# Another choice of scheduling rules per stretch of the plan, for a two-layer attention and MLP kernel on one core

## The chip, the cores and the metric

The kernel runs on one core of one Trainium2 chip. The metric is device microseconds of one execution, as the median of several. A core has five instruction queues that run in order and meet through semaphores: TensorE (PE, matmuls; its weight loads are listed as PEld), ScalarE (ACT, activation functions), VectorE (DVE), GpSimd (POOL) and SyncE (SP, which only issues DMAs here).

## The reference

Two rounds of attention and MLP over one sequence of S = 2048 tokens, D = 512, H = 32 heads of 16, F = 1792. Both rounds use the same weights.

```
x = x + A(layernorm(x));  x = x + B(layernorm(x))      # twice
A: qkv = x @ wqkv;  p = softmax(q k^T / 4) per head;  o = p v;  o @ wo
B: gelu(x @ w1 + b1) @ w2 + b2                           # tanh gelu
```

## The kernel before

**Cells.** The scores of one head for 128 keys and 512 queries are a *cell*: one 32-row matmul into one bank of PSUM (`score`, the lambda on line 1432). There are 4096 of them. A *pass* is a group of eight heads and 512 queries; its cells are numbered by key tile `kt` (16 of 128 keys) and by `a`, which names the row group of PE that holds the heads. No maximum is subtracted in the softmax: exp is taken of the scaled score directly.

**Two ways to take an exp.** ACT does it by its table, for two or three cells in one instruction (`exps`, line 1879). For some cells VectorE does it instead: one multiply-add whose 16-bit integer result is read as a bf16 (`dfirst`, line 1601), followed by two 64-bit additions on GpSimd (`dchain`, lines 1691 and 1695), which make shifted copies; the four copies are multiplied with V and three scaled copies of V (`VC`, line 1363) and summed. Which key tiles may go this way is in `KD` (line 52), five of sixteen in each layer. A cell of these five that VectorE has not been given by the end of its pass is taken by ACT (`next_act`).

**The rest.** Line 1945 multiplies the exps with V and collects the sums of the softmax in a 17th column; `norm` divides. Line 647 (`quads`) holds the matmuls of all projections and of the MLP. Line 1155 moves the MLP's hidden values from PSUM with their bias, line 1176 is the gelu on ACT (two long ones per query chunk, so that the table of ACT is switched to gelu and back once per chunk), and in the last chunk line 1150 takes gelu straight from PSUM. The projections and the MLP of a chunk of 512 tokens run beside the scores of the next chunk. Fillers are matmuls whose result nobody reads (`filler`); the planner puts them where PE would otherwise pause.

**What sets the order.** All of it is decided when the program is built. `_Sched.run` keeps a clock for each engine, and many threads (one for scores, one for exps, one for products with V, and so on) offer their next operation with an assumed duration and a priority. It picks the operation that can start first, notes its assumed end, and appends it to that engine's queue, with the semaphore waits that its data need. The chip then runs each queue in that order, at whatever speed it has; only the order is fixed.

**The rules.** Twelve constants of this planner are *knobs*. `ORDERS` (line 94) lists values for all twelve; `PICKS` names one line of it for each stretch of 24 us of the planner's ACT clock, 60 in all:

```
def tune(self):
    k = min(int(self.clock["act"] // STRETCH), len(PICKS) - 1)
    if k != self.stretch:
        self.stretch = k
        globals().update(zip(KNOBS, ORDERS[PICKS[k]]))
        LATENCY["pe"] = PE
```

The knobs in which the lines that are picked differ:

- `PE`: the assumed delay between a matmul's end and the start of what waits for it.
- `PTURG`: with fewer free buffers for exps than this, the products with V get a better priority (`urge`, line 1920).
- `PTLOW`: with more free buffers than this, the products with V take VectorE's cells first (line 1928).
- `SWAP`: how late VectorE may be while it is still given a cell in one of the two spare banks that a third cell of ACT's could use (`attach`, line 1534).
- `SEVAC`: the priority of VectorE's moves out of PSUM other than exps.
- `DULOW`: with no more free VectorE buffers than this, products with V are started although some rows have nothing yet (line 1917).

The other six are the same in all lines that are picked: `TOL` and `DCELL` in `attach`, `EXT` in `extend`, `ALONE` in `solo`, `TAIL` and `OPENING` in `next_d`. `attach` gives VectorE a cell only together with a group of ACT's, when a bank is free within `TOL`; `next_d` offers no more of a pass once fewer than `TAIL` of its cells are left.

Of the kernel before, what the change touches and what calls it, by code (L numbers as in the profile page):

```python
# [110 lines left out]
)  # L111
STRETCH = 24
PICKS = (1, 13, 1, 1, 13, 13, 1, 2, 1, 13, 1, 13, 13, 1, 1, 14, 1, 13, 13, 13, 13, 11, 3, 1,
         1, 13, 13, 13, 13, 13, 13, 1, 13, 13, 13, 1, 13, 1, 1, 1, 1, 3, 13, 13, 5, 1, 13, 13,
         1, 0, 1, 1, 13, 13, 13, 13, 1, 1, 1, 13)
LOG2E = 1.4426950408889634
E_SCALE = 0.25 * LOG2E * 128
E_BIAS = 15992.765054484162
# [145 lines left out]
class _Sched:  # L264
# [1793 lines left out]
```

## Time and profile before

| | us |
|---|---|
| median of 3 runs | 1429.57 (1429.56 to 1430.48) |
| profiled execution | 1429.75 |
| its span, first to last instruction | 1427.9 |
| ACT busy | 1401.1 (98%) |
| PE busy, fillers included | 1385.5 (97%) |
| VectorE busy | 1216.6 (85%) |
| GpSimd busy | 997.9 (70%) |

The profile is one execution, read from the hardware's own records. In a row of a group stand line, engine, operation, what it writes and reads with the shapes, how often, then busy time and mean duration of one, then the idle time of the engine just before these instructions and what ended it. Successive instructions of an engine overlap, so a mean duration can be longer than the step from one to the next. The chain of waits follows the work that ended last back to its releasers. A row of a stretch gives its borders and length, busy times with counts in brackets, the granted clock of TensorE (1.00 is full), the share of the DMA engines and GB/s.

### The profile page before, as it was taken

What the parts mean: (1) busy time and instruction counts of PE and PEld (TensorE: products, weight loads), DVE (VectorE), ACT (ScalarE), POOL (GpSimd) and SP (SyncE); (2) the same over time, 40 slices, a digit from 0 to 9 for tenths busy, and PEclk for the clock granted to TensorE, in tenths of its full rate; (3) what the DMA queues carried; (4) which work ended last, traced back from release to release, by engine and by line L of the source; (5) the groups of instructions that cost most, each with busy time, mean ns of one, the idle gap of its engine ahead of it and who ended that gap; (6) DMA issues with size and microseconds to landing.
All of it is one profiled execution on the core that took longest, in us unless ns stands there. A gap on an engine that the chain in (4) does not pass through costs nothing.

```text
span 1427.9 us, 45603 instructions
## 1 busy us (share of the span) xinstructions
PE 1385.5 (97%) x19402; PEld 420.7 (29%) x19402; DVE 1216.6 (85%) x2293; ACT 1401.1 (98%) x1406; POOL 997.9 (70%) x1256
## 2 busy tenths in 40 slices
PE   8999999999999999999999999999999999999999
PEld 3222222222222222222222222222222222344346
DVE  7789999788997889987998678899869977898684
ACT  7999999999999999999999999999999999999995
POOL 1086988668786787876767667757767977788661
PEclk9999999999999999999999999999999999999999
DMA  6100001261121611115411161101162105421522
GB/s 176 45 2 2 2 16 39 62 183 54 46 39 53 187 60 39 39 31 157 119 39 46 53 187 59 31 14 33 39 189 79 32 24 168 145 32 40 175 75 89
DMA packets 145187, 103.47 MB, mean 72 GB/s; under 512 B 37084, under 2 KB 143964, under 8 KB 144988
## 3 DMA queue, kind: packets, MB, share of 16 engines
q1 hardware_dynamic: 144988, 100.57, 25.2%
q8 instruction: 156, 2.56, 0.8%
q14 instruction: 43, 0.35, 0.1%
HBM read 88.74 MB, written 4.19 MB: 65 GB/s over the span
## 4 chain that ended last, share of the span: by engine, by line
ACT 67%; PE 24%; DVE 7%; POOL 2%; issue 1%; ACTq 0%; POOLq 0%
ACT pt L1879 50%; PE ps L1945 8%; PE ps L1432 8%; PE ps L647 7%; ACT q L1879 4%; ACT g L1879 3%; ACT g L1176 3%; ACT v L1879 3%; DVE du L1601 3%; ACT kt L1879 2%; POOL du L1695 1%; DVE kt L1601 1%; PE ps L1420 1%; ACT L1879 1%; ACT L1176 1%
## 5 line engine op out<-in xcount | busy, mean ns | idle before, releaser
L1879 ACT ACTIVATE pt<-ps 128x1024 bf16<-128x1024 f32 (+1 forms) x1085 | 1091.2, 1168 | 1.3 <-PE ps L1432 0.4
L1601 DVE TENSOR_SCALAR du<-ps 128x512 uint16<-128x512 f32 x894 | 597.2, 684 | 112.5 <-PE ps L1432 107.9
L1432 PE MATMUL ps<-qp,kt 32*128 32x512 bf16 x4096 | 537.4, 384 | 18.5 <-ACT pt L1879 11.2
L1695 POOL INT64_ADD du<-du x454 | 464.6, 1025 | 72.9 <-DVE qp L1380 9.6
L1691 POOL INT64_ADD du<-du x454 | 273.6, 605 | 231.9 <-DVE du L1601 180.8
L1945 PE MATMUL ps<-du,vc 128*17 128x512 bf16 (+1 forms) x2979 | 360.3, 360 | 2.3 <-POOL du L1695 0.6
L1432 PEld LDWEIGHTS ps<-qp,kt 32*128 32x128 bf16 x4096 | 143.2, 91 | 569.6 <-ACT pt L1879 177.9
L1945 PE MATMUL ps<-pt,v 128*17 128x512 bf16 (+1 forms) x2621 | 306.5, 359 | 4.3 <-ACT pt L1879 2.7
L1945 PE MATMUL ps<-du,v 128*17 128x512 bf16 (+1 forms) x993 | 166.3, 360 | 3.6 <-DVE v L988 1.0
L647 PE MATMUL ps<-xf,wr 128*32 128x512 bf16 (+1 forms) x2272 | 162.0, 371 | 0.4 <-DMA xf<-pt 0.2
L1601 DVE TENSOR_SCALAR kt<-ps 128x512 uint16<-128x512 f32 x202 | 136.2, 683 | 22.0 <-PE ps L1432 20.6
L1945 PE MATMUL ps<-kt,vc 128*17 128x512 bf16 (+1 forms) x732 | 145.1, 344 | 0.8 <-POOL du L1691 0.8
L1945 PEld LDWEIGHTS ps<-du,vc 128*17 128x17 bf16 x2979 | 95.6, 89 | 81.4 <-issue 35.6
L1695 POOL INT64_ADD kt<-kt x104 | 105.3, 1013 | 15.7 <-DVE ra L797 3.8
L647 PE MATMUL ps<-wr,g 128*32 128x512 bf16 x1504 | 110.7, 383 | 1.1 <-ACT g L1176 1.1
L1945 PEld LDWEIGHTS ps<-pt,v 128*17 128x17 bf16 x2621 | 74.2, 88 | 79.1 <-issue 53.2
L1945 PE MATMUL ps<-v,vc 128*17 128x512 bf16 (+1 forms) x405 | 90.4, 351 | 0.1
L1155 DVE TENSOR_SCALAR g<-ps,hb1t 128x512 bf16<-128x512 f32 (+1 forms) x112 | 79.0, 706 | 10.2 <-PE ps L647 9.8
L1601 DVE TENSOR_SCALAR v<-ps 128x512 uint16<-128x512 f32 x116 | 78.2, 682 | 11.0 <-PE ps L1432 10.6
L1691 POOL INT64_ADD kt<-kt x104 | 62.3, 599 | 35.6 <-DVE kt L1601 17.2
L1879 ACT ACTIVATE q<-ps 128x1024 bf16<-128x1024 f32 (+1 forms) x78 | 82.0, 1128 | 0.0
L1945 PE MATMUL ps<-kt,v 128*17 128x512 bf16 (+1 forms) x334 | 79.4, 354 | 1.9 <-POOL du L1695 0.9
(108 smaller groups left out, 1462.4 us busy)
## 6 DMA issues: line engine op xcount, KB each, us to landing
wr<-in_B_w_dram SPq DMA_DIRECT2D x243, 256.0 KB, 3.1
wr<-in_A_wqkv_dram SPq DMA_DIRECT2D x24, 256.0 KB, 2.8
wr<-in_A_wo_dram SPq DMA_DIRECT2D x17, 256.0 KB, 3.0
x<-in_A_x_dram SPq DMA_DIRECT2D x7, 512.0 KB, 4.9
pt<-in_B_w_dram SPq DMA_DIRECT2D x13, 256.0 KB, 3.9
kept<-x SPq DMA_DIRECT2D x4, 512.0 KB, 3.1
x<-kept SPq DMA_DIRECT2D x4, 512.0 KB, 3.9
out_dram<-x SPq DMA_DIRECT2D x16, 128.0 KB, 2.9
```

What stands on the lines that cost most here:

```text
L647: return [lambda e, a=a: e.matmul(out[32 * a:32 * a + 32, :], lhsT=lhsT[:, 32 * a:32 * a + 32], rhs=rhs, start=start, stop=stop, tile_posi ...
L1155: yield _Op("dve", 0.21 + n / 966, lambda e, fc=fc, pb=pb: e.tensor_scalar(T["G"][:, fc, q], pb, T["HB1T"][:, fc:fc + 1], None, op0=ALU.ad ...
L1176: lambda e, g=g: e.activation(out=g, in_=g, func=ACT.Gelu_apprx_tanh), reads=gk, writes=gk, prio=2)
L1420: fns.append(lambda e, o=o, w=w, a=a, m=m: e.matmul(o, lhsT=w, rhs=rhs, start=start, stop=start, tile_position=(0, m * a)))
L1432: return (lambda e: e.matmul(o, lhsT=lhsT, rhs=rhs, start=True, stop=True, tile_position=(32 * a, 0)), ["K%d.%d.%d" % (l, gb, kt // 4), "Q ...
L1601: yield _Op("dve", 0.682, lambda e: e.tensor_scalar(u, self.bank(b), E_SCALE, E_BIAS, op0=ALU.mult, op1=ALU.add), reads=["B.%d" % b], writ ...
L1691: yield _Op("pool", 0.151 + 0.2176 * n, lambda e: e.int64_add(words(1, 1), words(0, 1), SHIFT * ONES), reads=key[0], writes=key[1])
L1695: yield _Op("pool", 0.143 + 0.4352 * n, lambda e: e.int64_add(words(2, 2), words(0, 2), 2 * SHIFT * ONES), reads=key[0] + key[1], writes=k ...
L1879: yield _Op("act", 0.052 + 0.4267 * n, lambda e, src=src, dst=dst: e.activation(out=dst, in_=src, func=ACT.Exp, scale=0.25), reads=["B.%d" ...
L1945: op.fns.append(lambda e, o=o, lhsT=q[0][0][m], rhs=q[0][1][:, n * m:n * m + n], a=a, st=st, sp=sp: e.matmul(o, lhsT=lhsT, rhs=rhs, start= ...
```

## The change

Eight lines of `ORDERS` that no stretch picks are taken out, so the remaining ones get new numbers (old 5, 11, 13 and 14 become 4, 5, 6 and 7), and `PICKS` is replaced. By values, 31 of the 60 stretches get another rule than before: those numbered 1, 4, 5, 7, 10 to 15, 17, 21, 22, 24, 29, 30, 32, 33, 43 to 49 and 52 to 57. Rule 1 (`PE` 0.2175, `PTURG` 6) goes from 24 stretches to 31, and rule 6 (`PE` 0.219, `PTURG` 5) from 29 to 20. The new picks were found by running the program in order with disturbed durations of loads, matmul groups and gelus. Nothing else differs: no operation, shape, buffer or assumed duration of an operation.

```diff
     (0.219, 0.7, 99, 2, 0.2, 0.2, 6, 5, 0.68, 3.5, 10, 18),
-    (0.219, 0.45, 99, 2, 0.2, 0.2, 6, 5, 0.68, 3.5, 10, 18),
     (0.219, 0.55, 99, 2, 0.5, 0.2, 6, 5, 0.68, 3.5, 10, 18),
-    (0.219, 0.55, 99, 2, 0.35, 0.2, 6, 5, 0.68, 3.5, 10, 18),
-    (0.219, 0.55, 99, 2, 0.2, 0.1, 6, 5, 0.68, 3.5, 10, 18),
...
     (0.219, 0.55, 99, 2, 0.2, 0.2, 6, 4, 0.68, 3.5, 10, 18),
...
     (0.219, 0.55, 99, 2, 0.2, 0.2, 5, 5, 0.68, 3.5, 10, 18),
     (0.219, 0.55, 99, 1, 0.2, 0.2, 6, 3, 0.68, 3.5, 10, 18),
-    (0.2205, 0.6, 99, 2, 0.2, 0.2, 6, 5, 0.68, 3.5, 10, 18),
 )
 STRETCH = 24
-PICKS = (1, 13, 1, 1, 13, 13, 1, 2, 1, 13, 1, 13, 13, 1, 1, 14, 1, 13, 13, 13, 13, 11, 3, 1,
-         1, 13, 13, 13, 13, 13, 13, 1, 13, 13, 13, 1, 13, 1, 1, 1, 1, 3, 13, 13, 5, 1, 13, 13,
-         1, 0, 1, 1, 13, 13, 13, 13, 1, 1, 1, 13)
+PICKS = (1, 1, 1, 1, 1, 1, 1, 6, 1, 6, 5, 5, 1, 6, 6, 1, 1, 1, 6, 6, 6, 1, 6, 1,
+         5, 6, 6, 6, 6, 1, 1, 1, 1, 1, 6, 1, 6, 1, 1, 1, 1, 3, 6, 1, 6, 6, 3, 1,
+         3, 6, 1, 1, 5, 1, 3, 1, 6, 3, 1, 6)
```

The columns of a line are `PE, SWAP, EXT, DULOW, SEVAC, TOL, PTURG, PTLOW, DCELL, ALONE, TAIL, OPENING`.

4 rows, old and new, of the table ORDERS are left out of this document.

## The prediction

> **What bounds the kernel now.** I read four views in this order: the page's busy shares, three stages cut at the first and at the last exp, the groups that make up the exps on both engines, and eight stretches that each hold one eighth of the scores.
>
> ```profile
> span 1427.9 us, 45603 instructions
> PE 1385.5 (97%) x19402; PEld 420.7 (29%) x19402; DVE 1216.6 (85%) x2293; ACT 1401.1 (98%) x1406; POOL 997.9 (70%) x1256
> ```
>
> ACT and PE both look full, but PE is padded with matmuls put into its gaps (the fillers), so its share says little. The stages decide it:
>
> ```profile
> core 0: us, PE busy (x) PEld busy (x) DVE busy (x) ACT busy (x) POOL busy (x), PEclk, DMA share, GB/s
> 0.00:13.00 13.00, 9.51 (x163) 4.92 (x163) 7.78 (x29) 4.46 (x7) 3.83 (x16) 1.00 0.88 269
> 13.00:1401.40 1388.40, 1352.36 (x18669) 400.17 (x18672) 1197.48 (x2236) 1385.41 (x1383) 992.96 (x1238) 1.00 0.26 71
> 1401.40:1427.90 26.50, 23.59 (x577) 15.58 (x568) 11.34 (x30) 11.25 (x18) 1.15 (x2) 1.00 0.17 51
> ```
>
> Columns: the stretch and its length, each engine's busy time with its instructions, the granted clock, the DMA share. Between the first exp at 13.0 and the last at 1401.4, ACT is busy for 1385.41 of 1388.40 us: 2.99 us idle in 1388. So an order can shorten this stage in two ways only: give ACT less to do, or take some of these 3.0 us. Before it stand 13.0 us in which the first tiles are loaded, normalised and projected; behind it 26.5 us in which PE is busy for 23.59.
>
> **What ACT's work consists of, and what an order can move.** A cell is one 128x512 score matmul. An exp of it is done by ACT, two or three cells in one instruction, or by VectorE (L1601) with two additions on GpSimd (L1691, L1695).
>
> ```profile
> L1432 PE MATMUL ps<-qp,kt 32*128 32x512 bf16 x4096 | 537.4, 384 | 18.5 <-ACT pt L1879 11.2
> L1601 DVE TENSOR_SCALAR du<-ps 128x512 uint16<-128x512 f32 x894 | 597.2, 684 | 112.5 <-PE ps L1432 107.9
> L1601 DVE TENSOR_SCALAR kt<-ps 128x512 uint16<-128x512 f32 x202 | 136.2, 683 | 22.0 <-PE ps L1432 20.6
> L1601 DVE TENSOR_SCALAR v<-ps 128x512 uint16<-128x512 f32 x116 | 78.2, 682 | 11.0 <-PE ps L1432 10.6
> L1879 ACT ACTIVATE pt<-ps 128x1024 bf16<-128x1024 f32 x905 | 866.1, 1093 | 1.3 <-PE ps L1432 0.4 <-PE ps L1945 0.2
> L1879 ACT ACTIVATE pt<-ps 128x1536 bf16<-128x1536 f32 x179 | 258.6, 1546 | 0.0
> ```
>
> Of 4096 cells VectorE takes 894+202+116 = 1212, so ACT takes 2884. The code offers VectorE five key tiles of sixteen (KD, line 52), 5/16 x 4096 = 1280; 68 of these go back to ACT. That count is not fixed by the work: it is what the planner's order makes of it, and the rules in ORDERS act on it, on which bank is used, and on what PE does next.
>
> The price of a cell that changes engine comes from the chain of waits and from the groups inside two of its pieces (the mean durations above overlap one another, so they are no price):
>
> ```profile
> 1371.74 3.67 ACT g L1879 x4
> L1879 ACT ACTIVATE g<-ps 128x1024 bf16<-128x1024 f32 x4 | 3.8, 1085 | 0.0
> 905.02 9.10 ACT pt L1879 x9
> L1879 ACT ACTIVATE pt<-ps 128x1024 bf16<-128x1024 f32 x7 | 6.7, 1090 | 0.0
> L1879 ACT ACTIVATE pt<-ps 128x1536 bf16<-128x1536 f32 x2 | 2.8, 1494 | 0.0
> ```
>
> Four two-cell exps end 3.67 us after the exp before them: 0.918 us each, 0.459 a cell. Nine, of which two have three cells, take 9.10: (9.10 - 7 x 0.918) / 2 = 1.34 us, so a third cell adds 0.42. A cell moved costs or saves between 0.42 and 0.46 us of ACT; I take 0.45, as most are in pairs.
>
> The ScalarE: Activation LUTs page of the Trainium skill (What ACT_TABLE_LOAD costs) gives 186 ns + 0.833 ns an element, of which 93 ns overlap the next: 0.946 us for two cells, 0.473 a cell. This trace has 0.918, so the page would put every cell term below 3% higher; the measured step decides.
>
> **Eight equal shares of the scores.**
>
> ```profile
> 13.00:189.80 176.80, 84.97 (x132) 1.00 0.11 26
> 189.80:361.90 172.10, 106.94 (x162) 1.00 0.27 75
> 361.90:533.50 171.60, 104.87 (x157) 1.00 0.29 78
> 533.50:705.20 171.70, 105.64 (x159) 1.00 0.27 76
> 705.20:881.10 175.90, 99.09 (x147) 1.00 0.28 80
> 881.10:1057.90 176.80, 96.34 (x146) 1.00 0.17 48
> 1057.90:1227.20 169.30, 106.33 (x161) 1.00 0.32 91
> 1227.20:1401.40 174.20, 101.91 (x154) 1.00 0.34 95
> 13.00:189.80 176.80, 66.30 (x511) 1.00 0.11 26
> 1227.20:1401.40 174.20, 67.23 (x509) 1.00 0.34 95
> ```
>
> The first eight rows are VectorE's time on L1601 with the number of cells it took; the last two, PE on L1432, show that a stretch holds some 512 scores (all eight have 509 to 513). A full share for VectorE is 5/16 x 512 = 160. Four stretches have 162, 157, 159 and 161: at the cap, to within what straddles a border. Four are short: 132, 147, 146 and 154, together 61 cells. The lengths follow: three neighbours at 157 to 162 last 171.6 to 172.1, the ones at 146 and 147 last 176.8 and 175.9.
>
> **The change part by part.** Removing eight entries of ORDERS removes nothing that runs, since none of the eight is picked before. The new PICKS gives the same rule in 29 of the 60 stretches and another in 31; most of these swap two rules that differ in the assumed delay behind a matmul (0.2175 against 0.219 us) and in PTURG (6 against 5). No instruction's shape, no DMA and no table load is added or removed by the code; only who takes a cell, how cells are grouped, and the order within each engine. Four terms:
>
> - **Head, 13.0 us: 0.** The first of the 60 picks is the same before and after, and it covers the planner's first 24 us of ACT time.
> - **Cells on VectorE: taken as 0.** The trace of before can't show another order, so I bound it by the eight rows. The capped stretches can lose but hardly gain; their scatter is some 2 cells each. The four short ones can go either way. Their rows lie 6 to 28 below the cap, and the two neighbours at 147 and 146 differ by 1; I allow 4 each. Independent, that is an estimate of (4 x 2^2 + 4 x 4^2)^0.5 = 9 cells, 4 us, either way. The far ends: all 61 regained is -27 us; the four capped stretches falling to 146 is 55 cells, +25 us. Both are far from any mixture of rules this close to the old one, so I stay near the scatter.
> - **ACT waiting inside the long stage: -1.0 us.** Gain at most the 2.99 us. Loss: the nearest row is the wait of a gelu for its VectorE input, 1.2 us, which happens once, between the two half-wide gelus behind the last exp:
>
> ```profile
> L1176 ACT ACTIVATE g<-g 128x3584 bf16<-128x3584 bf16 x14 | 43.9, 3183 | 0.1
> L1176 ACT ACTIVATE g<-g 128x1792 bf16<-128x1792 bf16 x2 | 3.4, 1698 | 1.2 <-DVE g L1155 1.2
> L1176 ACT ACT_TABLE_LOAD x8 | 10.3, 1283 | 0.1
> L1879 ACT ACT_TABLE_LOAD x7 | 9.0, 1283 | 0.1
> ```
>
>  Eight gelu pairs with 1.2 us each would be +9.6. The disturbed durations named in the change aim at such waits, of which the long stage now has next to none (0.1 before the fourteen long gelus); I take a third of what is there, and keep -3.0 to +9.6.
> - **Tail, 26.5 us: 0.** PE is busy for 23.59 of it, so at most 2.9 can go. Two pieces of the chain of waits there, PE's last long runs of matmuls:
>
> ```profile
> 1404.94 5.37 PE ps L647 x96
> 1411.94 13.16 PE ps L647 x352
> ```
>
>  If a further group like the 96 slipped behind the last exp, it would add 5.4; I keep -2.9 to +5.4. The last two picks are the same rules as before; the three ahead of them differ.
>
> What hides the rest: VectorE's and GpSimd's own order costs nothing as long as ACT has a filled bank. If a VectorE cell comes late, its bank comes free late, the planner's next chance to give VectorE a cell is missed, and ACT takes that cell: the stall turns into the cell term above.
>
> Sum against the profiled execution: 1427.9 + 0 + 0 - 1.0 + 0 = 1426.9 of span. That execution took 1429.75 us, 1.85 more than its span, and the median of the runs is 0.18 below it, so 1426.9 + 1.85 - 0.18 = 1428.6 us. The measurement tells about 0.2% from no change, 2.9 us; -1.0 lies within it.
>
> **Rivals.**
>
> *Faster, cells regained.* VectorE waits for scores, so there is room in time:
>
> ```profile
> DVE du L1601 <- PE ps L1432: 107.9, 251, 4.5
> POOL du L1691 <- DVE du L1601: 180.8, 100, 53.0
> 144.00:168.00 24.00, 23.41 (x294) 5.94 (x286) 23.51 (x43) 23.96 (x27) 22.53 (x29) 1.00 0.01 2
> 168.00:192.00 24.00, 21.69 (x281) 5.64 (x277) 22.54 (x37) 23.85 (x26) 23.38 (x30) 1.00 0.01 2
> ```
>
> For it: 108 us of such waits in all, up to 4.5 us at once, and 61 cells short. Against it: in the shortest share, VectorE is busy for 23.51 and 22.54 of 24 us just where it catches up (last two rows, third engine), so its 28 are hard to regain and 33 remain in three other shares. A quarter of 61, 15 cells, is 6.8 us: 1422.8. It decides from 6.4 cells (2.9 / 0.45).
>
> *Slower, cells lost.* Place: stretches 43 to 57 of the planner, roughly 1032 to 1392 us, where thirteen of fifteen rules are others than before, and where two shares stand at 161 and 154. Mechanism: a bank that frees later than the planner's tolerance at a score group (TOL, SWAP in attach) gets no VectorE cell; at the end of a pass fewer than TAIL remain and ACT takes them. Price 0.45 a cell; it outweighs from 6.4 cells, and if those two shares fall to the 147 and 146 of their neighbours, 14 + 8 = 22 cells, it is 9.9 us; half of it, 11 cells with no gain elsewhere, is 5.0: 1434.6. For it: the capped shares can only fall. Against: nothing in the new rules makes VectorE's work dearer.
>
> *Slower, new waits on ACT.* Were every gelu pair to wait as the one does, +9.6 with nothing gained: 1439.2. Against it stands the 0.1 us.
>
> *No change to speak of.* If the cells stay at 1212 and waits at 3.0, it is another order with the same time, 1429.6; this lies in my own case.
>
> **Chances and range.** My case, within 0.2% (1426.7 to 1432.4): 0.45. Faster by regained cells 0.27. Slower by lost cells 0.22, by new waits or a longer tail 0.06. So faster 0.27, same 0.45, slower 0.28. The slower side is a little fuller than the scatter alone makes it, since four of eight shares are capped. The scatter of 4 us with 1.5 us for waits and tail gives 4.3, and 8 times in 10 that is 1.28 x 4.3 = 5.5 us each way: 1423.1 to 1434.1. I move the lower end to the faster rival's 1422.8 and the upper to 1435.5 for the capped shares. My own case alone is 1426.7 to 1432.4.
>
> **What would show it.** Count L1601: each cell away from 1212 should be 0.45 us of the long stage, so 1220 with the same waits reads 1426. The first exp should stand at 13.0, ACT's idle time between first and last exp at 1 to 3 us, the tail at 24 to 29, the table loads at 16. I am wrong in mechanism if the time moves by more than 2 us while L1601 stays within 3 cells of 1212 and ACT's idle time stays near 3.0, or if PE's granted clock leaves 1.00 inside the long stage.

## The result and the profile after

The changed kernel takes 1435.44 us (median of 5 runs, 1433.5 to 1436.8) against 1430.1 (5 runs, 1429.56 to 1430.48): 1.0037 times as long, 95% interval 1.0026 to 1.0048. A second measurement of the same program gave 1433.73 against 1429.65, 1.0029 (1.0017 to 1.0041). It is slower, by 4.1 to 5.3 us. The forecast was 1428.6, a gain, with a range whose upper end, 1435.5, is where the first measurement came out. The profiled execution took 1434.26 us.

The page's first lines and its groups after the change; the eight lines taken out of ORDERS move every later line number up by 8, so L1601 is now L1593, L1432 is L1424 and L1879 is L1871:

```profile
span 1432.4 us, 45480 instructions
PE 1386.2 (97%) x19362; PEld 420.5 (29%) x19362; DVE 1210.3 (84%) x2288; ACT 1404.2 (98%) x1409; POOL 992.4 (69%) x1242
L1593 DVE TENSOR_SCALAR du<-ps 128x512 uint16<-128x512 f32 x888 | 592.1, 682 | 97.2 <-PE ps L1424 92.5
L1593 DVE TENSOR_SCALAR kt<-ps 128x512 uint16<-128x512 f32 x199 | 133.5, 682 | 28.7 <-PE ps L1424 28.1
L1593 DVE TENSOR_SCALAR v<-ps 128x512 uint16<-128x512 f32 x120 | 80.9, 682 | 24.0 <-PE ps L1424 23.4
```

VectorE takes 888 + 199 + 120 = 1207 cells, five fewer than before. ACT takes these five: 2.3 us at 0.45. PE is as busy as before to within a microsecond, GpSimd and VectorE less. The three stages, cut again at the first and the last exp (length, then busy times of PE, PEld, DVE, ACT and POOL):

```profile
0.00:13.40 13.40, 9.13 (x163) 4.76 (x163) 7.67 (x29) 4.60 (x7) 3.83 (x16) 1.00 0.84 258
13.40:1405.50 1392.10, 1354.03 (x18672) 400.82 (x18671) 1191.52 (x2233) 1388.29 (x1385) 987.39 (x1224) 1.00 0.25 71
1405.50:1432.40 26.90, 23.06 (x540) 14.95 (x528) 11.16 (x28) 11.26 (x18) 1.15 (x2) 1.00 0.14 42
```

Against before, the head is 0.4 longer, the stage of the exps 3.7 (1392.10 against 1388.40), the tail 0.4: together 4.5, all of the span's growth. In the long stage ACT is busy for 2.9 us more (1388.29 against 1385.41) and idle for 0.8 more (3.8 against 3.0). Of the 2.9, five cells at 0.45 explain 2.3; the other 0.6 isn't traced. The clock is 1.00 in all three.

Where the cells went, in the same eight shares of some 512 scores (L1593, its time and count on VectorE; a cell on a border counts in both shares):

```profile
13.40:190.30 176.90, 84.90 (x132) 1.00 0.11 26
190.30:362.50 172.20, 107.07 (x162) 1.00 0.26 73
362.50:533.20 170.70, 107.24 (x161) 1.00 0.26 74
533.20:707.00 173.80, 101.44 (x152) 1.00 0.26 74
707.00:885.60 178.60, 97.15 (x146) 1.00 0.29 82
885.60:1062.00 176.40, 95.63 (x145) 1.00 0.18 51
1062.00:1231.70 169.70, 106.35 (x160) 1.00 0.32 93
1231.70:1405.50 173.80, 101.37 (x154) 1.00 0.33 96
```

The counts before were 132, 162, 157, 159, 147, 146, 161, 154. The third share gained four and is 0.9 us shorter; the fourth, one of those at the cap, fell from 159 to 152 and is 2.1 longer; the fifth, already short, is 2.7 longer at one cell less. The other five moved by 0.4 us at most. So the loss lies between 533 and 886 us. In the fourth share ACT is busy for 2.3 us more (173.63 against 171.31) and idles less; in the fifth it is busy for 2.1 more (177.61 against 175.50) and idles 0.6 more, which one cell doesn't explain.

### The profile page after: what moved, and what is told of

Its sections match the earlier page's. It is cut to its first block, busy times and chain, and to the rows that moved or that the text cites. A ratio compares the mean times of both kernels' runs of the same rounds, so it can differ in the third digit from the quotient of the medians.

```text
span 1432.4 us, 45480 instructions
## 1 busy us (share of the span) xinstructions
PE 1386.2 (97%) x19362; PEld 420.5 (29%) x19362; DVE 1210.3 (84%) x2288; ACT 1404.2 (98%) x1409; POOL 992.4 (69%) x1242
## 4 chain that ended last, share of the span: by engine, by line
ACT 68%; PE 20%; DVE 7%; POOL 2%; issue 1%; DMA 1%; SPq 0%; ACTq 0%; POOLq 0%
ACT pt L1871 50%; PE ps L1937 7%; PE ps L1424 7%; PE ps L639 6%; ACT q L1871 4%; ACT g L1871 4%; DVE du L1593 3%; ACT g L1168 3%; ACT kt L1871 3%; ACT v L1871 3%; POOL du L1687 1%; POOL du L1683 1%; DVE stats L771 1%; ACT L1871 1%; ACT L1168 1%
## 5 line engine op out<-in xcount | busy, mean ns | idle before, releaser
L1871 ACT ACTIVATE pt<-ps 128x1024 bf16<-128x1024 f32 (+1 forms) x1074 | 1080.5, 1167 | 2.2 <-PE ps L1424 1.2
L1593 DVE TENSOR_SCALAR du<-ps 128x512 uint16<-128x512 f32 x888 | 592.1, 682 | 97.2 <-PE ps L1424 92.5
L1424 PE MATMUL ps<-qp,kt 32*128 32x512 bf16 x4096 | 540.1, 384 | 23.1 <-ACT pt L1871 14.3
L1937 PE MATMUL ps<-du,vc 128*17 128x512 bf16 (+1 forms) x2970 | 352.0, 359 | 2.6 <-POOL kt L1683 1.1
L1424 PEld LDWEIGHTS ps<-qp,kt 32*128 32x128 bf16 x4096 | 144.8, 91 | 578.9 <-ACT pt L1871 185.2
L1937 PE MATMUL ps<-pt,v 128*17 128x512 bf16 (+1 forms) x2593 | 293.8, 359 | 5.1 <-ACT pt L1871 2.5
L1937 PE MATMUL ps<-du,v 128*17 128x512 bf16 (+1 forms) x990 | 163.1, 359 | 3.1 <-DVE v L980 1.6
L1593 DVE TENSOR_SCALAR kt<-ps 128x512 uint16<-128x512 f32 x199 | 133.5, 682 | 28.7 <-PE ps L1424 28.1
L1937 PE MATMUL ps<-kt,vc 128*17 128x512 bf16 (+1 forms) x711 | 139.8, 347 | 0.3 <-POOL kt L1683 0.3
L1937 PEld LDWEIGHTS ps<-du,vc 128*17 128x17 bf16 x2970 | 91.0, 89 | 78.0 <-issue 36.9
L1593 DVE TENSOR_SCALAR v<-ps 128x512 uint16<-128x512 f32 x120 | 80.9, 682 | 24.0 <-PE ps L1424 23.4
L1871 ACT ACTIVATE q<-ps 128x1024 bf16<-128x1024 f32 (+1 forms) x85 | 88.9, 1124 | 0.0
L1937 PE MATMUL ps<-v,vc 128*17 128x512 bf16 (+1 forms) x420 | 84.4, 350 | 0.0
```

Source lines behind the costliest of these rows:

```text
L1424: return (lambda e: e.matmul(o, lhsT=lhsT, rhs=rhs, start=True, stop=True, tile_position=(32 * a, 0)), ["K%d.%d.%d" % (l, gb, kt // 4), "Q ...
L1593: yield _Op("dve", 0.682, lambda e: e.tensor_scalar(u, self.bank(b), E_SCALE, E_BIAS, op0=ALU.mult, op1=ALU.add), reads=["B.%d" % b], writ ...
L1871: yield _Op("act", 0.052 + 0.4267 * n, lambda e, src=src, dst=dst: e.activation(out=dst, in_=src, func=ACT.Exp, scale=0.25), reads=["B.%d" ...
L1937: op.fns.append(lambda e, o=o, lhsT=q[0][0][m], rhs=q[0][1][:, n * m:n * m + n], a=a, st=st, sp=sp: e.matmul(o, lhsT=lhsT, rhs=rhs, start= ...
```

## The experiments

Two theories stood against each other. *Work*: the new order makes ACT do more, because fewer cells reach VectorE; its price is 0.45 us a cell, and the waits matter little. *Wait*: the new order makes ACT wait more on this chip. Later came a third question: what the disturbed runs that chose the picks have bought. All experiments are built on the code of before, so their lines have its numbers (7 more behind the loads where a helper was added).

| kernel | cells on VectorE | median us | before beside it | ratio (95%) |
|---|---|---|---|---|
| after_again | 1207 | 1433.73 | 1429.65 | 1.0029 (1.0017 to 1.0041) |
| b48a | 1212 | 1430.89 | 1429.65 | 1.0008 (0.9999 to 1.0017) |
| a24b | 1207 | 1434.54 | 1429.65 | 1.0034 (1.0022 to 1.0047) |
| all3 | 1183 | 1459.85 | 1429.65 | 1.0208 (1.0194 to 1.0222) |
| more_cells | 1215 | 1429.34 | 1430.08 | 0.9994 (0.9985 to 1.0002) |
| all13 | 1205 | 1435.27 | 1430.08 | 1.0033 (1.0021 to 1.0045) |
| mild_before | 1212 | 1450.76 | 1429.84 | 1.0145 (1.0123 to 1.0168) |
| mild_after | 1207 | 1446.41 | 1429.84 | 1.0114 (1.0101 to 1.0128) |
| dist_before | 1212 | 1552.62 | 1430.08 | 1.0861 (1.0836 to 1.0887) |
| dist_after | 1207 | 1540.7 | 1430.08 | 1.0771 (1.0757 to 1.0785) |
| dist_more | 1215 | 1549.76 | 1429.84 | 1.0837 (1.0817 to 1.0857) |
| dist_all13 | 1205 | 1545.76 | 1429.84 | 1.0807 (1.0789 to 1.0826) |

Four of these kernels give results that differ from the reference's: a24b, all13 and dist_all13 by a relative error of 0.105, all3 by 0.049. Their traces still hold 4096 scores, and exps for 4096 cells, like the others', so their times are used here as those of orders of the same work; what goes wrong in them isn't known, and they could not replace the kernel.

**The changed kernel again** (the old table with the new picks written in its numbers; no instruction differs).

> The changed kernel once more, with the full table of rules, so that its lines have the numbers of before; the order is the same instruction for instruction. Work theory (ACT is dearer because fewer cells go to VectorE): L1601 again 1207 cells, 5 fewer than before, 2.3 us; ACT's idle and stretched time between first and last exp within 1 us of the first profile, and the runs 1433.5 to 1436.8. Wait theory (the new order makes ACT wait on the chip): the waits behind 109 us differ from execution to execution by 1 to 3 us and make up the rest of the 5 us. If the profile is shorter or longer than the first by over 1 us before 109 us, where the order is still that of before, that part belongs to the execution and not to the order.

The stages of this second execution:

```profile
0.00:12.00 12.00, 8.39 (x163) 4.55 (x163) 7.64 (x29) 4.50 (x8) 3.84 (x16) 1.00 0.83 254
12.00:1404.00 1392.00, 1354.06 (x18668) 400.82 (x18671) 1191.86 (x2233) 1388.24 (x1385) 988.70 (x1224) 1.00 0.25 71
1404.00:1431.20 27.20, 22.92 (x540) 15.01 (x532) 11.21 (x28) 11.30 (x19) 1.15 (x2) 1.00 0.14 42
```

The long stage repeats to 0.1 us (1392.00, ACT busy 1388.24, idle 3.8). The head doesn't: 12.0 against 13.4, though it runs the same instructions in the same order. So the 3.6 to 3.7 us of the long stage belong to the order, and a microsecond of head comes and goes with the execution. The wait theory's swings of 1 to 3 us didn't show.

**Where in the run it arises.** Two mixtures of the old and new picks:

```diff
 b48a:  PICKS = before[:48] + after[48:]
 a24b:  PICKS = after[:24] + before[24:]
```

> Rules of before in stretches 0 to 47, rules of after from 48 on. The plan gives VectorE 1212 cells, as before. Work theory: within 1.5 us of before, 1430 to 1431.5. Wait theory with the cause in the late rules: 1433 or more at the same number of cells.

> Rules of after in stretches 0 to 23, rules of before from 24 on. The plan gives VectorE 1207 cells, as after. Work theory: 5 x 0.45 = 2.3 us over before and up to 1 us more, 1432 to 1434. Wait theory with the cause in the early rules: 1434 to 1437, as after; with the cause in the late rules: 1430 to 1432.

Long stage of b48a, then of a24b:

```profile
12.90:1401.90 1389.00, 1352.70 (x18691) 399.95 (x18694) 1197.54 (x2237) 1385.77 (x1381) 993.84 (x1234) 1.00 0.25 71
```

```profile
12.30:1404.80 1392.50, 1357.45 (x18696) 401.98 (x18699) 1191.21 (x2231) 1388.11 (x1385) 990.20 (x1228) 1.00 0.25 71
```

With the same 1212 cells, the late picks cost 1.2 us in the median (interval from nothing to 2.4), 0.6 of it in this stage; that is the work theory's 1430 to 1431.5. The early picks alone, with the old ones behind them, cost all of it: ACT busy 2.7 more than in before, idle 4.4 against 3.0. The time, 4.9 over before, is above what I expected from work alone (2 to 4) and within what the wait theory had for the early rules (1434 to 1437): the order that loses the cells also waits more. An order can't be taken apart freely here, since every later choice starts from another state; after stretch 24 this is not the order of before any more, though its rules are.

**A large lever.** Rule 3 everywhere.

```diff
-PICKS = (1, 13, 1, ...)
+PICKS = (3, 3, 3, ...)
```

> Rule 3 (SWAP 0.7) in all stretches: VectorE may be later and still be given a cell, at the cost of ACT's third bank. The plan gives VectorE 1183 cells, 29 fewer than before. Work theory: 29 x 0.45 = 13 us over before, 1443, with ACT's waits within 3 us of before's. Wait theory: the cells are a side matter, and the time follows ACT's idle time; at most 5 us over before if that stays near 3 us.

Its long stage and tail, and then ACT's largest wait (total, times, longest):

```profile
12.30:1428.40 1416.10, 1372.74 (x18691) 409.56 (x18694) 1171.13 (x2202) 1401.08 (x1383) 970.71 (x1208) 1.00 0.25 69
1428.40:1457.70 29.30, 26.16 (x665) 18.21 (x653) 13.81 (x36) 11.21 (x18) 1.15 (x2) 0.99 0.37 109
```

```profile
ACT pt L1879 <- PE ps L1432: 10.6, 7, 6.8
```

30 us slower, where work alone gave 13 and the wait theory at most 5. ACT is busy 15.7 us more, of which 29 cells explain 13; it idles 15.0 us instead of 3.0, most of that for scores (10.6 us in seven waits, one of 6.8); and the tail is 2.8 longer. So both theories are half right: fewer cells on VectorE is the part that can be counted, and this order, which loses many of them, also leaves ACT without scores. For the change itself the split is about 2.3 to 2.9 of work to 0.8 of idle time.

**More cells.** Four picks other than before's, found by building varied plans without running them and taking the one whose own ACT clock ends first.

```diff
 picks of before, but 23: 10, 56: 12, 58: 0, 59: 14
```

> The picks of before with four stretches changed (23, 56, 58 and 59), chosen among varied picks because the program, when built, gives VectorE most cells at the least end of its own ACT clock: 1215 cells, 3 more than before, and an ACT clock that ends 1.4 us earlier. Work theory: 1 to 1.5 us under before, 1428.2 to 1428.7. Wait theory: this order was chosen without regard to disturbances just as before was, so its waits may eat the gain: 1429.5 to 1432.

```profile
12.80:1400.20 1387.40, 1353.63 (x18672) 399.90 (x18671) 1199.18 (x2239) 1384.50 (x1382) 995.28 (x1240) 1.00 0.25 71
```

Three more cells, ACT busy 0.9 us less, the long stage 1.0 shorter, idle time as before. The median is 0.7 lower than that of before beside it, but the interval of the ratio holds 1; a gain of this size isn't shown by the runs, only by the stage of one execution. The 1429.34 lies in neither of the two expected ranges.

**One rule everywhere.** Rule 13 in all 60 stretches, an order that nobody chose stretch by stretch.

> Rule 13 (PE 0.219, PTURG 5; number 6 in the changed table) in all stretches. VectorE gets 1205 cells, 7 fewer than before and 2 fewer than after; the program's own ACT clock ends 4.2 us later than before's. Work theory: 7 x 0.45 = 3.2 us for the cells and about 1 us of waits that stand in the plan already: 1433 to 1434.5, much like after. Wait theory (a choice of rules stretch by stretch by disturbed runs saves waits that one rule everywhere has): 2 us or more above after, 1436 or later, with the difference in ACT's waits and not in cells.

```profile
13.20:1406.50 1393.30, 1355.71 (x18685) 400.77 (x18688) 1188.25 (x2229) 1389.57 (x1383) 988.30 (x1226) 1.00 0.25 70
```

1435.27, between the two expected ranges and level with after (1435.44 and 1433.73), with ACT idle 3.7 us, where after has 3.8. So undisturbed, the new picks save no waits over one rule everywhere.

**What the plan itself says.** Three ends of each order: the planner's ACT clock behind its last operation, its last exp, and the last exp in the profile (the two executions of after both):

| | before | after | b48a | a24b | all3 | more_cells | all13 |
|---|---|---|---|---|---|---|---|
| planner's ACT clock at its end | 1402.2 | 1405.2 | 1403.4 | 1405.6 | 1426.3 | 1400.7 | 1406.4 |
| last exp ends in the plan | 1382.7 | 1385.8 | 1383.2 | 1386.1 | 1405.3 | 1381.4 | 1386.2 |
| last exp ends in the profile | 1401.4 | 1405.5, 1404.0 | 1401.9 | 1404.8 | 1428.4 | 1400.2 | 1406.5 |

The first and the last row lie within 2.1 us of each other, but that is a coincidence: the planner's clock ends with the gelus behind the last exp. Exp against exp, the plan is 18.2 to 23.1 us short. What it gets right is the difference between orders. Against before, its last exp moves by 3.1 us in after, 0.5 in b48a, 3.4 in a24b, 22.6 in all3, -1.3 in more_cells and 3.5 in all13; the profile's moves by 4.1 and 2.6, 0.5, 3.4, 27.0, -1.2 and 5.1. So some 3 us were in the plan of after already. The picks of before stand at a low point of that clock: of 633 plans that I built with one to three of its picks varied at random, 196 give VectorE fewer cells, 416 as many and 21 more, and three end earlier, by 1.2 us at most. (These are counts in plans, not runs.) Few other choices can gain anything here, and disturbed runs chose by another measure.

**What the disturbed runs have bought.** Ahead of each weight load of the ring the SyncE queue issues a DMA between two DRAM places that no instruction of the work waits for, so that the loads land late; the order of all else is kept. The copies are extra work that changes no result. There are 302 of them, not 284 as the expectations say. With 128 KB the program also waits for the copies behind its output.

```diff
-yield _Op("sp", WCOST, lambda e: e.dma_start(dst, src), ...
+yield _Op("sp", WCOST, [self.spare, lambda e: e.dma_start(dst, src)], ...
```

> The order of before, and ahead of each of the 284 weight loads of the ring a second DMA of 512 KB between two DRAM places, which nothing waits for: the loads land later, the queues hold the same order otherwise. Taken with the next kernel. Work theory: the disturbance costs both orders about the same, and this one stays 3 to 5 us ahead. Robustness theory (the new picks are better once loads are disturbed): this order loses 3 us or more over the other by the disturbance, so that it is level or behind.

> The order of after with the same 284 extra DMAs. Work theory: 3 to 5 us above the disturbed order of before. Robustness theory: level with it or below it.

The issues of the weights in before (the last column is the median time to landing):

```profile
wr<-in_B_w_dram SPq DMA_DIRECT2D x243, 256.0 KB, 3.1
```

With 512 KB, the same, PE's wait for them and the long stage in dist_before, then in dist_after:

```profile
wr<-in_B_w_dram SPq DMA_DIRECT2D x243, 256.0 KB, 7.6
```

```profile
PE ps L647 <- DMA wr<-in_B_w_dram: 62.2, 61, 2.8
```

```profile
13.20:1524.40 1511.20, 1401.72 (x18659) 399.13 (x18659) 1201.19 (x2236) 1398.99 (x1383) 995.29 (x1238) 0.96 0.51 167
```

```profile
wr<-in_B_w_dram SPq DMA_DIRECT2D x243, 256.0 KB, 7.6
```

```profile
PE ps L647 <- DMA wr<-in_B_w_dram: 55.3, 52, 2.6
```

```profile
12.10:1507.90 1495.80, 1392.08 (x18660) 399.02 (x18663) 1192.93 (x2232) 1399.60 (x1385) 989.41 (x1224) 0.97 0.52 170
```

The loads land in 7.6 us (median) instead of 3.1, and now the order of after is the faster one, by 11.9 us. It still does more on ACT (1399.60 against 1398.99), but ACT idles for 96 us of the long stage in it and for 112 in the order of before. (The profiled execution of dist_before took 1557.31 us, 4.7 over its median, so its 112 us are somewhat high.) My work theory, which had the gap of 3 to 5 us stay, fell here. How much of the gap is waits for weights isn't separated: PE waits 6.9 us less for them in the order of after, and at the clocks of 0.97 and 0.96 its matmuls of the long stage also take 9.6 us less (1392.08 against 1401.72).

Two controls with the same 512 KB, and the pair with 128 KB:

> The order of more_cells, picked without disturbances, with the 512 KB DMAs. If the new picks are better under late loads because disturbed runs chose them: this one stands with the disturbed order of before, 1548 to 1558. If orders scatter by 10 us under such a disturbance whatever chose them: anywhere from 1538 to 1560, and a time near 1541 speaks for chance.

> One rule in all stretches, with the 512 KB DMAs; an order that nothing chose. If disturbed runs chose well: above 1548, like the disturbed order of before. If chance: anywhere from 1538 to 1565.

> The order of before with an extra 128 KB DMA ahead of each weight load in place of 512 KB, so that the loads land about 1 us later instead of 4.5 (estimate: a quarter of what the 512 KB did). Insurance theory (the new picks pay 3 to 4 us of work for less loss when loads are late): the gap to the next kernel shrinks in proportion, 4 - 16/4 = 0, so the two are within 1.5 us of each other. Threshold theory (the buffers of weights hide small delays in both orders): this stays 3 to 5 us ahead.

> The order of after with the extra 128 KB DMAs. Insurance theory: within 1.5 us of the order of before with the same DMAs. Threshold theory: 3 to 5 us above it.

The landing of the weights, PE's wait for them and the long stage in mild_before, then in mild_after:

```profile
wr<-in_B_w_dram SPq DMA_DIRECT2D x243, 256.0 KB, 4.4
```

```profile
PE ps L647 <- DMA wr<-in_B_w_dram: 14.7, 24, 1.3
```

```profile
12.30:1420.70 1408.40, 1357.38 (x18659) 397.63 (x18659) 1198.51 (x2236) 1389.19 (x1383) 993.13 (x1238) 1.00 0.33 97
```

```profile
wr<-in_B_w_dram SPq DMA_DIRECT2D x243, 256.0 KB, 4.3
```

```profile
PE ps L647 <- DMA wr<-in_B_w_dram: 9.2, 17, 1.4
```

```profile
12.30:1418.80 1406.50, 1358.35 (x18668) 399.43 (x18671) 1192.80 (x2233) 1391.61 (x1384) 987.30 (x1224) 1.00 0.33 98
```

Loads that land 1.3 us later are enough to take the lead from the order of before: 1450.76 for it, 1446.41 for that of after, with ACT idle 19.2 and 14.9 us in the long stage, and PE waiting 14.7 and 9.2 us for weights. That the order of after leads at this size isn't settled: the runs of the two overlap (1447.2 to 1454.6, 1444.9 to 1448.2), and so do the intervals of their ratios. Both of my numbers for this pair missed: I had them level or the order of before ahead.

With 512 KB the four orders stand at 1552.62 (before), 1549.76 (more_cells), 1545.76 (one rule) and 1540.7 (after). The two whose undisturbed plans end first are the slowest, the one rule lies between, and the one chosen by disturbed runs is the fastest. I had put the one rule above 1548 if disturbed runs chose well, so a part of the 11.9 us is that before does worse than an unchosen order, 6.9, and the rest, 5.1, that after does better than one. Only the lead of after is free of overlap: its longest run took 1541.7, the shortest of the others 1542.4. Four orders are too few to tell choice from luck.

So once loads land 4.5 us later the order of after is the faster one, and the undisturbed chip doesn't call for it. In the profile of before, the loads land in 3.1 us, and no wait of PE for a weight load of the ring stands among its waits of 0.2 us or more. The picks were chosen with matmul groups and gelus disturbed as well; no run here disturbs those.

## Why the prediction was wrong, point by point

- **Views and bound: right.** ACT is the bound, before and after; the span's growth of 4.5 us is 3.7 of the exps' stage, 0.4 of head and 0.4 of tail. Of the signs set down, the tail and the 16 table loads came as said; ACT's idle time, 3.8 us, lies outside the 1 to 3.
- **Head, taken as 0: right for the order, too firm as a number.** The order is the same up to 109 us, but the first exp came at 12.0 to 13.4 us in the six undisturbed executions that begin with the same order (before, after twice, b48a, a24b, more_cells).
- **Cells, taken as 0: the step that failed.** I read a scatter of 9 cells either way out of the eight shares and put the middle at no change. It is five fewer, 2.3 us, inside that scatter but the largest single term of the loss. What the rows had told was one-sided: four shares at the cap. I wrote that down, widened the range for it, and left the middle where it was.
- **Waits, taken as -1.0: the second failure, and the one that made the sign.** I let the aim of the change stand for an effect. ACT's idle time rose by 0.8 us, to the level of the order with one rule everywhere. Late loads, which the picks guard against, were no wait of PE in the trace of before, and I had quoted the row that said the same for the gelus (0.1 us). A guard against a wait that isn't there had nothing to win here.
- **Tail, taken as 0: about right.** 26.9 and 27.2 against 26.5.
- **Rival "cells lost": right in sign and in its term, wrong in place and size.** That a bank comes free too late for the planner was its reason; no trace shows why the cells were lost. I placed it at 1032 to 1392 us of the planner's clock, where most rules differ. There the counts stayed within one, and the late picks alone (b48a) cost about 1 us. The cells went at 533 to 707, and the time at 533 to 886. The time wasn't lost where the rules differ most; each choice passes a new state to the next, which may be why. Its 1434.6 us lies between the two measurements by luck: it had eleven cells in it, and the measured times five cells, 0.6 us of ACT's work that isn't traced, 0.8 of idle time and a longer head and tail.
- **Price of a cell, 0.45: about right.** ACT's busy time rose by 2.9 us for five cells, 0.58 each, fell by 0.9 for three, 0.30 each, and rose by 15.7 for 29, 0.54 each. It wasn't enough for the time of all3, where ACT's idle time grew by 12 us beside that.

## What to carry to other kernels

When only an order changes, count first what the bounding engine is given to do, then its idle time: here 3.0 us of idle time was all that could be won from waits, and of 633 other plans only 21 gave VectorE more cells. An order made robust against late data can have a price, 4.1 to 5.3 us here, so look first whether the trace shows waits for late data; and an order that leads by 4 us in quiet conditions lost that lead when loads landed 1.3 us later. Where a program plans its own order, its clock can compare orders before the chip is used, like operation against like: here the shift of the last exp was right within 1.6 us for five orders and 4.4 us short for the one that lost most cells, while the end itself was 18 to 23 us short.

## What the runs showed of the hardware that was not expected

An extra 128 KB in front of each 256 KB load, with the DMA engines busy for a third of the time, made the loads land 1.3 us later and the order of before 21 us slower (1450.76 against 1429.84), although the weight ring has five buffers or more. With 512 KB, the granted clock's mean was 0.96 and 0.97 in the long stage (dist_before and dist_after), where it is 1.00 in all undisturbed orders, and PE was busy 49 and 38 us longer for the same work; what brought the clock down isn't shown. The head varies more than the long stage: in two executions of the same program the first exp came at 13.4 and 12.0 us, while the 1392 us behind it agreed within 0.1.
